# Logarithms first in the common ScalarE stretch: reordering one round of a fused RWKV, Mish and routed-expert kernel

## The chip, the cores and the metric

The kernel runs on one core of a Trainium2 chip. Its time is the device time of one execution in microseconds (us). A kernel's figure is the median of its timed runs. One further execution was recorded by the hardware profiler, and every row below comes from that one.

The engines in the rows are PE (TensorE, matmul), PEld (its weight loads), DVE (VectorE), ACT (ScalarE), POOL (GpSimd) and SP (SyncE, which issues most DMAs). Each works through its own instructions strictly in the order in which they stand in the program, and they meet only at semaphores.

## The reference

Three layers follow each other. The sizes are batch 4, 8 heads, sequence 768, head size 48, so 3072 tokens of 384 numbers.

```python
# 1. attention with a decaying state
for t in range(S):
    cur = np.einsum('bhd,bhe->bhde', u[None] * kt, vt)
    y[:, :, t] = np.einsum('bhd,bhde->bhe', rt, state + cur)
    state = wt[:, :, :, None] * state + np.einsum('bhd,bhe->bhde', kt, vt)
# 2. a dense layer of 2048 with h * tanh(softplus(h)) between
h = x @ w_in
sp = np.where(h > 20.0, h, np.log1p(np.exp(np.minimum(h, 20.0))))
x = (h * np.tanh(sp)) @ w_out
# 3. 8 experts, each token to one, at most 384 per expert, greedy by logit
logits = x @ w_gate
out[mask] = np.maximum(x[mask] @ w1[e], 0.0) @ w2[e]
```

## The kernel before

**Tiling.** The attention works on 24 units of 128 columns (two chunks of 64 tokens). The dense layer works on 12 groups g of 256 tokens, two units each. A group's first matmul (`mm1`) has 8 slots of 18 matmuls; each slot fills one PSUM tile `Hp`, and there are two of these. ScalarE takes a slot out of PSUM twice: as a sigmoid into `es` and scaled into `hs`. A few of the `hs` copies are on VectorE. The second matmul (`mm2`, into `X`) is cut into parts of three matmuls, and the number of parts that go into a slot stands in a list (`beat`).

**The activation.** tanh(softplus(h)) is made from the sigmoid by an arctangent over half a group (`act_ln`, 128x2048) and a sine over each quarter (`act_tanh`, 128x1024). VectorE multiplies the sine into `hs` (L594, the sine product). Then `act_g` splits the product into two halves of 16 bits, `ghi` (copy) and `glo` (rest, L607), which `mm2` reads.

**The attention unit.** Steps of unit n, each a function: `att0` multiplies up the decay along the tokens (a scan into `E`) and makes `rk`; `att_inv` forms 1/E on ScalarE as Ln and Exp; `att1` scales r; `att1b` improves the inverse by one Newton step and scales k by it (L410, L411 and L414, the result is `k1` and lies in the tile `T`); `att_K` transposes k1 on PE (L447) and copies it to `kn`; `att_A` multiplies k1 by r1 and the state by r1 (L430, L436) and a predicated copy puts the first into `Dt`; `att_S` makes the new state from `kn` (L465, L472, L474); `att4` closes the output (L487) and writes it split into `xg` (hi on ScalarE, lo on VectorE, L494), which `mm1` of a later group reads. `bon1` and `bon2` make the diagonal term with small matmuls.

**The order.** No scheduler decides it. Every step gets a number from `CFG`, the steps are sorted by it, and each engine's instructions stand in that order. Slot t has its `mm1` at t + 0.7 and its `mm2` parts at t + 1.275. In the middle of the kernel one group is one round of 8 slots; T stands for the number of a round's first slot. At T both halves of the group just finished have their sines in one place, which is called the common stretch here, and the Ln and Exp of two units stand there too. ScalarE evaluates functions from a table, and an ACT_TABLE_LOAD changes the table. The sigmoid and the arctangent share one table in this order, the sine takes another, and Ln and Exp a third. `att_inv` asks for its table for each unit. Nine of the ten common stretches (groups 1 to 9) hold Ln and Exp of two units, the tenth (group 10) none.

The buffers that matter: `hs` and `es` are two half-group tiles each, `E` two tiles (one per unit in turn), `Hp` two PSUM banks, `Y` (transposes, states, diagonal terms) two, and `A` one.

Of the kernel before, what the change touches and what calls it, by code (L numbers as in the profile page):

```python
# [9 lines left out]
F32 = mybir.dt.float32  # L10
F16 = mybir.dt.float16
I32 = mybir.dt.int32
AF = mybir.ActivationFunctionType
ALU = mybir.AluOpType
# [4 lines left out]
P = 128  # L19
# [4 lines left out]
CFG = {'conv': [-27.9, -26.2, -0.2, 0.8, 1.8, 2.8, 3.7, 5.3, 5.9, 6.6, 7.3, 8.0, 8.7, 10.4, 10.6, 11.3],  # L24
 'split': [-27.3, -25.6, 0.9, 1.9, 2.9, 3.8, 4.7, 5.6, 6.7, 7.4, 8.1, 8.8, 9.0, 11.2, 11.4, 12.1],
 'ogT': [7.4, 8.45, 9.9, 10.25, 10.95, 11.85, 12.55, 12.75],
 'ogM': [8.15, 9.35, 10.2, 10.9, 11.35, 11.95, 12.75, 13.95],
 'u': ({'att0': -3.6, 'bon1': -2.6, 'bon2': -1.6, 'inv': 0.22, 'r1': 0.23, 'k1': 0.24, 'K': 2.6, 'A1': 2.8,
        'S': 3.99, 'y': 4.0},
       {'att0': -1.5, 'bon1': -0.6, 'bon2': 1.6, 'inv': 0.25, 'r1': 0.26, 'k1': 3.1, 'K': 4.4, 'A1': 4.6,  # L30
        'S': 5.79, 'y': 5.8}),
 'un': {0: {'att0': -17.25,
            'inv': -16.75,
            'r1': -16.55,
# [53 lines left out]
            'k1': 4.3,  # L88
            'K': 5.9,
            'A1': 6.2,  # L90
            'S': 7.45}},
 'rate': [(9, 0), (16, 19), (80, 195), (82, 200), (85, 216), (89, 218), (93, 234), (99, 258)],
 'beat': (16, 80, (5, 4, 2, 2, 2, 1, 1, 5)),
 'close_cv': 15.0,
 'close_att': 86.65,
 'mm1': 0.7,
# [1 line left out]
 'aln': -0.1,  # L98
 'tanh': (1.475, 1.66),
 'g': (3.0, 3.0725),  # L100
 'both': (((0.1, 0.11), (0.105, 0.115)), ((0.12, 0.13), (3.2, 3.6))),
 'begin': {('warm', 0): -32,
           ('wg',): 5.6,
           ('ld', 4): -23.99,
# [66 lines left out]
         'ghi': {2, 6} | {i for i in range(8, 46) if i % 4 != 3},  # L171
         'hs': {64, 17, 55, 60, 63},
         'rk': {0, 1, 2, 3, 5, 6, 7, 9, 10, 11, 12, 13, 14, 15, 16, 17, 18, 19, 20, 21, 22, 23},
         'x0': set(),
         'bT': {22},
         'wT': {4}},
 'nd0': 8,
 'lg2': 4.725,
 'alone': {9},
 'lg': 4.51,  # L180
 'hold': 30}


# [1 line left out]
def tile_rwkv_mish_greedy_moe(  # L185
# [12 lines left out]
    nc = tc.nc  # L198
    NU, C, H, D = v.shape
    L = C // 2  # L200
# [4 lines left out]
    NP = H // 2  # L205
    F2 = w1.shape[2] * P // DM
    KD = DM // P
    NF = FF // P
    NS = NF // 2
    NF2 = F2 // P  # L210
    G = 256
    NG = NT // G
# [5 lines left out]
    SX, SWI, SG, SWO = 2.0**14, 2.0**10, 2.0**13, 2.0**11  # L218
# [16 lines left out]
    pm = p_moe.__enter__()  # L235
    pa = p_att.__enter__()
    pc = p_cv.__enter__()
# [68 lines left out]
    right = const.tile([P, 1], F32, name="right")  # L306
# [4 lines left out]
    first = pa.tile([P, 2 * NP, L + 1], F32, name="first", bufs=1)  # L311
    nc.gpsimd.memset(first, 0.0)
    nc.gpsimd.memset(first[:, :, 0:1], 1.0)
    full = pa.tile([P, P], I32, name="full", bufs=1)
    nc.gpsimd.memset(full, 1)
    nc.gpsimd.affine_select(out=full, in_=full, pattern=[[1, P]], compare_op=ALU.is_gt, fill=0,
                            base=0, channel_multiplier=-1)
# [16 lines left out]
    made = set()  # L334

    def need(*keys):
        assert made.issuperset(keys), keys

    def on_v(what, i):
        return i in CFG["dve"].get(what, ())  # L340

    def move(what, i, dst, src, scale=1.0):
        if on_v(what, i):
            nc.vector.tensor_scalar(dst, src, scale, None, op0=ALU.mult)
        else:
            nc.scalar.activation(dst, src, AF.Copy, scale=scale)  # L346

    def E_of(n):
        return E_buf[n % 2]
# [19 lines left out]
    def att_inv(n):  # L369
        need(("att0", n))  # L370
        inv = pa.tile([P, 2 * NP, L], F32, name="inv", bufs=2)
        if n > 1:
            nc.scalar.preload_act_table_set("natural_log_exp_and_others")
        nc.scalar.activation(inv, E_of(n)[:, :, 1:], AF.Ln)
        nc.scalar.activation(inv, inv, AF.Exp, scale=-1.0)
        st[n] = inv
# [29 lines left out]
    def att1b(n):  # L406
        E = E_of(n)
        inv, r1 = st[n]
        nt = pa.tile([P, 2 * NP, L], F32, name="nt", bufs=1)
        (nc.vector if on_v("nt", n) else nc.gpsimd).tensor_tensor(nt, inv, E_of(n)[:, :, 1:], op=ALU.mult)  # L410
        nc.vector.scalar_tensor_tensor(inv, nt, 2.0, inv, op0=ALU.subtract, op1=ALU.mult)  # L411
        k1 = Tps["k", n]
        kk = k1.rearrange("q p (h t) -> q (p h) t", h=2)
        nc.vector.scalar_tensor_tensor(kk, inv, -1.0, kk, op0=ALU.mult, op1=ALU.mult)  # L414
        st[n] = (k1, r1, None)
        made.add(("k1", n))
# [140 lines left out]
    hs, es, gs = {}, {}, {}  # L557
    HALF = NF // 4

    def mm1(g, j):  # L560
        need(("w", j), ("y", MG * g), ("y", MG * g + MG - 1))
        hf, q = divmod(j, HALF)
        if q == 0:
            hs[g, hf] = pm.tile([P, NF // 2, G], F32, name="hs", bufs=2)
            es[g, hf] = pm.tile([P, NF // 2, G], F32, name="es", bufs=2)
        made.add(("mm1", g, hf, q))
        h = pp.tile([P, 2, G], F32, name="Hp", bufs=2)
        for fi in range(2):
            f = 2 * j + fi
            n = 0  # L570
            for kk in range(KD):
                for a, b in ((0, 0), (0, 1), (1, 0)):
                    nc.tensor.matmul(h[:, fi, :], wi[:, a, kk, f * P:(f + 1) * P], xg[g][:, b, kk, :],  # L573
                                     start=(n == 0), stop=(n == 3 * KD - 1))
                    n += 1
        nc.scalar.activation(es[g, hf][:, 2 * q:2 * q + 2, :], h, AF.Sigmoid, scale=-1.0 / (SX * SWI))  # L576
        move("hs", g * NS + j, hs[g, hf][:, 2 * q:2 * q + 2, :], h, SG / (SX * SWI))

    def act_ln(H_):
        e = es[divmod(H_, 2)]  # L580
        need(("mm1", *divmod(H_, 2), HALF - 1))
        made.add(("at", H_))
        nc.scalar.activation(e, e, AF.Arctan)  # L583

    def act_tanh(H_, q):
        key = divmod(H_, 2)
        sl = slice(q * NF // 4, (q + 1) * NF // 4)
        h, e = hs[key][:, sl], es[key][:, sl]
        need(("at", H_))
        made.add(("sin", H_, q))  # L590
        if q == 0 and not (H_ % 2 and 0 < H_ // 2 < NG - 1):
            nc.scalar.preload_act_table_set("trig_and_small")
        nc.scalar.activation(e, e, AF.Sin, scale=-2.0, bias=right)  # L593
        nc.vector.tensor_tensor(h, h, e, op=ALU.mult)  # L594

    def act_g(H_, q):
        key = divmod(H_, 2)
        if q == 0:
            pool = pg3[0] if key[0] >= NG - 2 else (p_g, pg2[0])[key[0] // 2 % 2]
            gs[key] = pool.tile([P, 2, NF // 2, G], F16, name="g")  # L600
        gt = gs[key]
        made.add(("g", *key, q))
        need(("sin", H_, q))
        sl = slice(q * NF // 4, (q + 1) * NF // 4)
        h = hs[key][:, sl]
        move("ghi", 2 * H_ + q, gt[:, 0, sl], h)
        (nc.vector if on_v("glo", 2 * H_ + q) else nc.gpsimd).tensor_tensor(gt[:, 1, sl], h, gt[:, 0, sl], op=ALU.subtract)  # L607

# [78 lines left out]
    def at(key, f, *args):  # L687
        events.append((key, len(events), f, args))
# [4 lines left out]
    for f in range(NF):  # L693
        at(CFG["ogT"][f // 2], og_T, f)
        if f % 2 == 0:
            at(CFG["ogM"][f // 2], og_M, f)
    steps = {"att0": att0, "bon1": bon1, "bon2": bon2, "inv": att_inv, "r1": att1, "k1": att1b, "A1": att_A, "K": att_K, "S": att_S, "y": att4}
    for n in range(NU):
        own = CFG["un"].get(n)
        t0 = 8 * (n // 2) - 8 if own is None else 4 * n - 13  # L700
        for nm, o in (CFG["u"][n % 2] if own is None else own).items():
            at(t0 + o, steps[nm], n)
    nc.sync.dma_start(wg.rearrange("p k e -> p (k e)"), w_gate)
    warm_rhs = first.rearrange("p a c -> p (a c)").bitcast(F16)[:, 0:512]
# [50 lines left out]
    for t in range(NSLOT + 3):  # L755
        if t < NSLOT:
            at(t + CFG["mm1"], mm1, t // NS, t % NS)
        at(t + CFG["mm2"], mm2, t)
    for h in range(NSLOT // 4):
        t = 4 * h + 4  # L760
        at(t + CFG["aln"], act_ln, h)
        tanh, g = CFG["tanh"], CFG["g"]
        if 0 < h // 2 < NG - 1:
            t = 8 * (h // 2) + 8
            tanh, g = CFG["both"][h % 2]
        for q in range(2):
            at(t + tanh[q], act_tanh, h, q)
            at(t + g[q], act_g, h, q)
        if h % 2 and ND0 <= h // 2 < NG - 1:
            at(t + CFG["lg"], logits, h // 2)  # L770
            at(t + CFG["lg2"], logits_sum, h // 2)
# [16 lines left out]
    for i, o in enumerate(OFF + [1.0]):  # L788
        t = pgt.tile([P, J], F32, name=f"jk{i}")
# [32 lines left out]
    y = pgt.tile([P, NTT], F32, name="y")  # L822
# [215 lines left out]
    sl = pgt.tile([P, NTT], I32, name="sl")  # L1038
# [269 lines left out]
```

## Time and profile before

| what | us |
|---|---|
| median of 3 runs | 928.54 (926.84 to 928.73) |
| profiled execution, whole | 925.72 |
| its span (the rows' time axis) | 924.0 |
| PE busy | 777.9 (84%) |
| VectorE busy | 541.5 (59%) |
| ScalarE busy | 473.8 (51%) |
| GpSimd busy | 64.2 (7%) |

The span is what all rows count from. The busy shares are means over stages with different limits: loading and the first groups (0 to 149 us), nine rounds with a common stretch that holds Ln and Exp (149 to 560), the last groups and the routing (to about 710), the experts (the rest). The granted clock of PE is given in shares of 2.4 GHz: 1.00 is full, 0.50 is 1.2 GHz.

### The profile page before, as it was taken

The page shows a single profiled execution, that of the slowest core. Times are in us where ns is not written, and L with a number is a line of the kernel's source. Part 1 is how long each engine was busy: PE and PEld are TensorE (multiplying, and loading weights), DVE is VectorE, ACT ScalarE, POOL GpSimd, SP SyncE. Part 2 cuts the span into 40 slices and gives each one's busy share as a digit, 9 for nine tenths or more (in the row PEclk, how much of TensorE's full clock was granted, in tenths as well). Part 3 has the DMA queues.
Part 4 walks back from the last instruction along what each step waited for, and adds up shares of the span by engine and source line. Part 5 has one row for each costly group of instructions (what it writes and reads, how often), then busy time and mean ns, then how long its engine had stood idle before and what let it go on. Part 6 is the DMA issues. An engine that isn't in the chain of part 4 may idle for free. (4 is left out here: it accounts for less than half of the span.)

```text
span 924.0 us, 20138 instructions
## 1 busy us (share of the span) xinstructions
PE 777.9 (84%) x8819; PEld 531.1 (57%) x8819; DVE 541.5 (59%) x946; ACT 473.8 (51%) x694; POOL 64.2 (7%) x102
## 2 busy tenths in 40 slices
PE   6873887787878888797979697999995999999997
PEld 3553665565656656565657475755554555555564
DVE  7799855556565655666656535267775455554430
ACT  3357966574747474847384836721101454554421
POOL 1000000000000000000000000100002022233311
PEclk8797999798979898989989899999997999999999
DMA  7840511303030303031302000040042455544300
GB/s 287 261 133 5 172 27 23 70 14 70 14 70 23 70 14 70 14 67 26 79 14 46 13 11 13 10 155 19 18 152 65 154 180 188 174 146 161 127 27 26
DMA packets 22220, 74.12 MB, mean 80 GB/s; under 512 B 4496, under 2 KB 13072, under 8 KB 20080
## 3 DMA queue, kind: packets, MB, share of 16 engines
q1 hardware_dynamic: 19056, 63.35, 23.3%
q0 software_dynamic: 3072, 9.44, 3.2%
q8 instruction: 71, 1.16, 0.5%
q14 instruction: 21, 0.17, 0.1%
HBM read 62.15 MB, written 9.44 MB: 77 GB/s over the span
## 5 line engine op out<-in xcount | busy, mean ns | idle before, releaser
L573 PE MATMUL Hp<-xg,wi 128*128 128x256 f16 x1728 | 229.2, 292 | 9.1 <-ACT hs L346 5.7
L621 PE MATMUL X<-wo,g 128*128 128x392 f16 (+1 forms) x1152 | 214.2, 330 | 0.6 <-ACT wT L346 0.6
L573 PEld LDWEIGHTS <-wi 128*128 128x128 f16 x1728 | 177.8, 105 | 47.4 <-issue 7.6
L576 ACT ACTIVATE es<-Hp 128x512 f32<-128x512 f32 x96 | 57.5, 599 | 168.5 <-PE Hp L573 168.4
L621 PEld LDWEIGHTS <-g 128*128 128x128 f16 x1152 | 106.4, 98 | 64.2 <-issue 1.4
L594 DVE TENSOR_TENSOR hs<-hs,es 128x1024 f32<-128x1024 f32 x48 | 57.5, 1221 | 83.4 <-ACT es L593 83.4
L1153 PE MATMUL Hp<-xe,a 128*128 128x384 f16 (+1 forms) x612 | 100.9, 316 | 6.4 <-DVE hT L1158 5.2
L1170 PE MATMUL X<-a,hT 128*128 128x384 f16 x576 | 97.2, 326 | 0.0
L1153 PEld LDWEIGHTS <-a 128*128 128x128 f16 x612 | 57.6, 97 | 48.2 <-issue 14.2
L1170 PEld LDWEIGHTS <-hT 128*128 128x128 f16 x576 | 56.4, 98 | 34.8
L447 PE MATMUL Y<-ident,T 128*128 128x128 f32 x88 | 19.0, 353 | 62.3 <-DVE T L414 54.9
L1158 DVE SCALAR_TENSOR_TENSOR hT<-Hp,hT 128x384 f16<-128x384 f32 x64 | 35.3, 552 | 46.6 <-ACT hT L1157 46.6
L1099 DVE SCALAR_TENSOR_TENSOR a<-stg,a 128x1024 f16<-128x1024 f32 (+4 forms) x56 | 59.6, 1065 | 3.3 <-ACT a L1096 2.7
L607 DVE TENSOR_TENSOR g<-hs,g 128x1024 f16<-128x1024 f32 x48 | 57.9, 1224 | 5.1 <-ACT g L346 4.0
L1096 ACT ACTIVATE a<-stg 128x1024 f16<-128x1024 f32 (+4 forms) x56 | 51.1, 926 | 6.6 <-DMA stg<-in_w_dram 6.6
L346 ACT ACTIVATE hs<-Hp 128x512 f32<-128x512 f32 x91 | 54.2, 596 | 0.1
L1173 ACT ACTIVATE or<-X 128x384 f32<-128x384 f32 x24 | 11.8, 491 | 81.3 <-issue 61.0
L447 PEld LDWEIGHTS Y<-ident,T 128*128 128x128 f32 x88 | 12.6, 178 | 69.5 <-DVE T L414 58.4
L593 ACT ACTIVATE es<-es,right 128x1024 f32<-128x1024 f32 x48 | 51.7, 1138 | 0.2
L1135 DVE SCALAR_TENSOR_TENSOR xe<-cn,xe 128x384 f16<-128x384 f32 x24 | 13.3, 555 | 60.8 <-ACT xe L1134 60.8
L1157 ACT ACTIVATE hT<-Hp 128x384 f16<-128x384 f32 x64 | 31.4, 491 | 32.6 <-PE Hp L1153 31.5
L583 ACT ACTIVATE es<-es 128x2048 f32<-128x2048 f32 x24 | 45.9, 1912 | 0.1
(194 smaller groups left out, 922.4 us busy)
## 6 DMA issues: line engine op xcount, KB each, us to landing
stg<-in_w_dram SPq DMA_DIRECT2D x16, 1536.0 KB, 7.3
T<-in_rkw_dram SPq DMA_DIRECT2D x42, 289.5 KB, 5.0
v<-in_v_dram SPq DMA_DIRECT2D x24, 192.0 KB, 2.9
raw<-in_w_out_dram SPq DMA_DIRECT2D x6, 768.0 KB, 4.6
x_dram<-x1o SPq DMA_DIRECT2D x48, 96.0 KB, 2.2
wo<-in_w_in_dram SPq DMA_DIRECT2D x4, 768.0 KB, 8.2
raw<-in_w_in_dram SPq DMA_DIRECT2D x2, 768.0 KB, 7.7
g<-in_w_in_dram SPq DMA_DIRECT2D x2, 768.0 KB, 10.5
```

The lines of the kernel that those rows point to most:

```text
L346: nc.scalar.activation(dst, src, AF.Copy, scale=scale)
L573: nc.tensor.matmul(h[:, fi, :], wi[:, a, kk, f * P:(f + 1) * P], xg[g][:, b, kk, :], start=(n == 0), stop=(n == 3 * KD - 1))
L576: nc.scalar.activation(es[g, hf][:, 2 * q:2 * q + 2, :], h, AF.Sigmoid, scale=-1.0 / (SX * SWI))
L583: nc.scalar.activation(e, e, AF.Arctan)
L593: nc.scalar.activation(e, e, AF.Sin, scale=-2.0, bias=right)
L594: nc.vector.tensor_tensor(h, h, e, op=ALU.mult)
L607: (nc.vector if on_v("glo", 2 * H_ + q) else nc.gpsimd).tensor_tensor(gt[:, 1, sl], h, gt[:, 0, sl], op=ALU.subtract)
L621: nc.tensor.matmul(x, gt[:, a, ff, m * P:(m + 1) * P], wo[:, b, f, 0:n], start=(f == 0 and i == 0), stop=(f == NF - 1 and i == 2))
L1096: nc.scalar.activation(dst[:, 0], src, AF.Copy, scale=sc_)
L1099: nc.vector.scalar_tensor_tensor(dst[:, 1], src, sc_, dst[:, 0], op0=ALU.mult, op1=ALU.subtract)
L1153: nc.tensor.matmul(ps[:, cs], a1[:, a, kk, f * P:(f + 1) * P], x[:, b, kk, cs], start=(n == 0), stop=(n == 3 * KD - 1))
L1170: nc.tensor.matmul(ps, h[:, a, f, ms], a2[:, b, f, :], start=(n == 0), stop=(n == 3 * NF2 - 1))
```

## The change

- In the common stretch the Ln and Exp of both units come first, on one table load; then one load of the sine's table, under which the arctangent of the second half now runs as well; then the four sines.
- On VectorE, `att1` and `att1b` of both units stand ahead of the four sine products. The products of the first half come next, those of the second half at T + 2.45 and T + 2.5, and the splits (`g`) are spread from T + 1.33 to T + 4.7.
- `att_K` and `att_A` of the first unit move from T + 2.6 and 2.8 (behind the second slot) to T + 1.28 and 1.3 (behind the first), its `att_S` and `att4` from about 4 to 2.4, and the second unit's steps from 4.4 to 5.8 to 3.3 to 4.6. `att0`, `bon1` and `bon2` of the next round's units move with them.
- `hs` becomes five tiles of a quarter group. To make room, the Newton product `nt` is written over the first 64 columns of `E`, and `full` goes to another pool.
- Five `hs` copies go from VectorE to ScalarE, most `kn` copies of even units from ScalarE to VectorE, and `beat` moves one `mm2` part from the second slot of a round to the sixth.

```diff
- 'u': ({'att0': -3.6, 'bon1': -2.6, 'bon2': -1.6, 'inv': 0.22, 'r1': 0.23, 'k1': 0.24, 'K': 2.6, 'A1': 2.8,
-        'S': 3.99, 'y': 4.0},
-       {'att0': -1.5, 'bon1': -0.6, 'bon2': 1.6, 'inv': 0.25, 'r1': 0.26, 'k1': 3.1, 'K': 4.4, 'A1': 4.6,
-        'S': 5.79, 'y': 5.8}),
+ 'u': ({'att0': -5.0, 'bon1': -3.1, 'bon2': -2.1, 'inv': 0.1, 'r1': 0.101, 'k1': 0.102, 'K': 1.28, 'A1': 1.3,
+        'S': 2.39, 'y': 2.4},
+       {'att0': -2.8, 'bon1': -1.9, 'bon2': -0.8, 'inv': 0.11, 'r1': 0.111, 'k1': 0.112, 'K': 3.3, 'A1': 3.4,
+        'S': 4.59, 'y': 4.6}),
...
- 'beat': (16, 80, (5, 4, 2, 2, 2, 1, 1, 5)),
+ 'beat': (16, 80, (5, 3, 2, 2, 2, 2, 1, 5)),
...
- 'both': (((0.1, 0.11), (0.105, 0.115)), ((0.12, 0.13), (3.2, 3.6))),
+ 'both': ((0.12, (0.14, 0.15), (1.33, 2.75)), (0.13, (2.45, 2.5), (3.6, 4.7))),
...
-        if n > 1:
+        if n > 1 and (n < 6 or n % 2 == 0):
             nc.scalar.preload_act_table_set("natural_log_exp_and_others")
...
-        nt = pa.tile([P, 2 * NP, L], F32, name="nt", bufs=1)
+        nt = E[:, :, 0:L]
...
         if q == 0:
-            hs[g, hf] = pm.tile([P, NF // 2, G], F32, name="hs", bufs=2)
             es[g, hf] = pm.tile([P, NF // 2, G], F32, name="es", bufs=2)
+        if q % 2 == 0:
+            hs[g, hf, q // 2] = pm.tile([P, NF // 4, G], F32, name="hs", bufs=5)
...
     def act_ln(H_):
         e = es[divmod(H_, 2)]
         need(("mm1", *divmod(H_, 2), HALF - 1))
         made.add(("at", H_))
+        if H_ % 2 and 0 < H_ // 2 < NG - 1:
+            nc.scalar.preload_act_table_set("trig_and_small")
         nc.scalar.activation(e, e, AF.Arctan)
...
+            at(t0 + sin, act_sin, h, 0, 1)
+            for q in range(2):
+                at(t0 + he[q], act_he, h, q)
+                at(t0 + g[q], act_g, h, q)
```

The next three places show what stands in a row on one engine, all of the round of group 6, which in the trace of before begins at 376.7 us. In the changed program the line numbers are a few higher (L594 becomes L605, L447 becomes L449).

ScalarE before, from the sigmoid of the group's last slot to the load that gives the sigmoid its table back:

```order
L576 ACTIVATE es<-Hp 128x512
L583 ACTIVATE es<-es 128x2048
L592 ACT_TABLE_LOAD
L593 ACTIVATE es<-es,right 128x1024 x4
L373 ACT_TABLE_LOAD
L374 ACTIVATE inv<-E_134 128x512
L375 ACTIVATE inv<-inv 128x512
L373 ACT_TABLE_LOAD
L374 ACTIVATE inv<-E_137 128x512
L375 ACTIVATE inv<-inv 128x512
L576 ACT_TABLE_LOAD
```

ScalarE of the changed program, the same place (`hs` is the copy that was on VectorE):

```order
L579 ACTIVATE es<-Hp 128x512
L348 ACTIVATE hs<-Hp 128x512
L375 ACT_TABLE_LOAD
L376 ACTIVATE inv<-E_134 128x512
L377 ACTIVATE inv<-inv 128x512
L376 ACTIVATE inv<-E_137 128x512
L377 ACTIVATE inv<-inv 128x512
L587 ACT_TABLE_LOAD
L588 ACTIVATE es<-es 128x2048
L597 ACTIVATE es<-es,right 128x1024 x4
L579 ACT_TABLE_LOAD
```

Four table loads become three, and both units' Ln and Exp stand ahead of the arctangent and the sines instead of behind them.

VectorE before, from the first sine product to the second unit's scaled r (T_89 and T_90 are the tiles of the two units):

```order
L594 TENSOR_TENSOR hs<-hs,es 128x1024
L344 TENSOR_SCALAR g<-hs 128x1024
L607 TENSOR_TENSOR g<-hs,g 128x1024
L594 TENSOR_TENSOR hs<-hs,es 128x1024
L344 TENSOR_SCALAR g<-hs 128x1024
L607 TENSOR_TENSOR g<-hs,g 128x1024
L594 TENSOR_TENSOR hs<-hs,es 128x1024 x2
L382 TENSOR_TENSOR T_89<-T_89,E_134 128x512
L410 TENSOR_TENSOR nt<-inv,E_134 128x512
L411 SCALAR_TENSOR_TENSOR inv<-nt,inv 128x512
L414 SCALAR_TENSOR_TENSOR T_89<-inv,T_89 128x512
L382 TENSOR_TENSOR T_90<-T_90,E_137 128x512
```

VectorE of the changed program, from the first unit's scaled r to the copy of its transposed k1:

```order
L384 TENSOR_TENSOR T_89<-T_89,E_134 128x512
L412 TENSOR_TENSOR E_134<-inv,E_134 128x8x64
L413 SCALAR_TENSOR_TENSOR inv<-E_134,inv 128x512
L416 SCALAR_TENSOR_TENSOR T_89<-inv,T_89 128x512
L384 TENSOR_TENSOR T_90<-T_90,E_137 128x512
L412 TENSOR_TENSOR E_137<-inv,E_137 128x8x64
L413 SCALAR_TENSOR_TENSOR inv<-E_137,inv 128x512
L416 SCALAR_TENSOR_TENSOR T_90<-inv,T_90 128x512
L605 TENSOR_TENSOR hs<-hs,es 128x1024 x2
L346 TENSOR_SCALAR x1o<-X 128x384
L640 TENSOR_SCALAR V<-X 128x8
L346 TENSOR_SCALAR kn<-Y 128x512
```

The three instructions of each unit's k1 stand ahead of all sine products, and `kn` stands behind two of them.

PE before, at the transposes of the first unit's k1 (12 `mm2` matmuls stand ahead of them, 18 `mm1` matmuls behind):

```order
L621 LDWEIGHTS g
L621 MATMUL X<-wo,g 128x392
L447 MATMUL Y<-ident,T_89 128x128 x4
L573 LDWEIGHTS wi
L573 MATMUL Hp<-xg,wi 128x256
```

PE of the changed program, at the same transposes, which stand one slot earlier:

```order
L449 MATMUL Y<-ident,T_89 128x128 x4
L432 MATMUL A<-T_89 64x64 x16
L438 MATMUL A<-T_89,S_135 64x64 x16
L576 LDWEIGHTS wi
L576 MATMUL Hp<-xg,wi 128x256
```

The products `A` now follow the transposes directly, and the next `mm1` is that of the round's second slot instead of its third.

## Rows read from the trace of the kernel before

**Rows 1.** Waits of PE, 148 to 560 us: total us, times, longest

```profile
PE Y L447 <- DVE T L414: 54.9, 9, 7.8
```

**Rows 2.** Round of group 6 and all nine: length, engines' busy us, clock, DMA

```profile
379.28:423.80 44.52, 36.44 (x510) 27.14 (x509) 29.52 (x43) 26.66 (x37) 1.33 (x1) 0.92 0.23 48
...
sum 411.03, PE 331.24 PEld 246.12 DVE 238.47 ACT 250.66 POOL 1.33; mean PE 36.80 PEld 27.35 DVE 26.50 ACT 27.85 POOL 0.15
```

**Rows 3.** Timeline of ScalarE, round of group 6: start, us, instruction, idle before

```profile
377.35 1.91 ACT L583 ACTIVATE es<-es 128x2048 f32<-128x2048 f32 x1
...
380.57 4.27 ACT L593 ACTIVATE es<-es,right 128x1024 f32<-128x1024 f32 x4
384.86 1.28 ACT L373 ACT_TABLE_LOAD   x1
386.15 0.63 ACT L374 ACTIVATE inv<-E 128x512 f32<-128x512 f32 x1
...
387.46 1.28 ACT L373 ACT_TABLE_LOAD   x1
...
391.36 0.60 ACT L576 ACTIVATE es<-Hp 128x512 f32<-128x512 f32 x1
391.86 0.59 ACT L346 ACTIVATE hs<-Hp 128x512 f32<-128x512 f32 x1
```

**Rows 4.** Timeline of PE, same round

```profile
376.52 2.65 PE L621 MATMUL X<-wo,g 128*128 128x392 f16 x15
379.01 2.13 PE L573 MATMUL Hp<-xg,wi 128*128 128x256 f16 x18
380.97 2.65 PE L621 MATMUL X<-wo,g 128*128 128x392 f16 x15
...
393.07 1.12 PE L447 MATMUL Y<-ident,T 128*128 128x128 f32 x4 [5.39 <-DVE T L414]
393.98 4.05 PE L573 MATMUL Hp<-xg,wi 128*128 128x256 f16 x18
397.96 0.80 PE L430 MATMUL A<-T 48*64 48x64 f32 x32
...
399.16 1.17 PE L621 MATMUL X<-wo,g 128*128 128x392 f16 x6
...
402.22 0.68 PE L465 MATMUL Y<-v,kn 64*64 64x48 f32 x32
402.73 0.63 PE L487 MATMUL A<-Dt,v 64*48 64x64 f32 x32
...
418.70 0.43 PE L392 MATMUL Y<-rk,u_T 128*32 128x64 f32 x16 [0.78 <-DVE rk L366]
```

**Rows 5.** Timeline of VectorE, same round

```profile
381.75 1.23 DVE L594 TENSOR_TENSOR hs<-hs,es 128x1024 f32<-128x1024 f32 x1 [3.71 <-ACT es L593]
...
383.74 1.23 DVE L607 TENSOR_TENSOR g<-hs,g 128x1024 f16<-128x1024 f32 x1
...
390.88 0.69 DVE L410 TENSOR_TENSOR nt<-inv,E 128x512 f32<-128x512 f32 x1
...
405.01 0.61 DVE L472 TENSOR_TENSOR S<-S,Y 128x192 f32<-128x192 f32 x2
...
406.13 0.75 DVE L494 SCALAR_TENSOR_TENSOR xg<-A,xg 128x256 f16<-128x256 f32 x2
406.79 0.68 DVE L344 TENSOR_SCALAR kn<-Y 128x512 f32<-128x512 f32 x1
407.39 1.23 DVE L363 TENSOR_TENSOR_SCAN E<-T,first 128x520 f32<-128x520 f32 x1
...
409.12 0.72 DVE L438 COPY_PREDICATED Dt<-mask,A 128x512 f32<-128x512 int32 x1
```

**Rows 6.** PE in single microseconds: length, busy (instructions), clock, DMA share, GB/s

```profile
180.00:181.00 1.00, 1.00 (x26) 0.50 0.47 107
...
391.00:392.00 1.00, 0.00 (x0) 0.71 0.00 0
...
404.00:405.00 1.00, 0.46 (x3) 1.00 0.51 123
```

More of the change, by code (lines that the diff above doesn't have):

```diff
@@ L90 @@
             'A1': 6.2,
-            'S': 7.45}},
+            'S': 7.45},
+        6: {'att0': -3.6, 'bon1': -2.7, 'bon2': -0.9},
+        7: {'att0': -1.4, 'bon1': -0.6, 'bon2': -0.4}},
  'rate': [(9, 0), (16, 19), (80, 195), (82, 200), (85, 216), (89, 218), (93, 234), (99, 258)],
- 'beat': (16, 80, (5, 4, 2, 2, 2, 1, 1, 5)),
+ 'beat': (16, 80, (5, 3, 2, 2, 2, 2, 1, 5)),
  'close_cv': 15.0,
@@ L168 @@
          'Dt': {0, 1, 2, 3, 4, 5, 6, 7, 8, 9, 10, 11, 12, 13, 14, 15, 16, 18, 19, 20, 21, 22, 23},
[1 row of a table removed]
[1 row of a table added]
          'x1': {2, 3, 5, 7, 8},
-         'ghi': {2, 6} | {i for i in range(8, 46) if i % 4 != 3},
-         'hs': {64, 17, 55, 60, 63},
+         'ghi': {2} | {i for i in range(4, 46) if i % 4 != 3},
+         'hs': set(),
          'rk': {0, 1, 2, 3, 5, 6, 7, 9, 10, 11, 12, 13, 14, 15, 16, 17, 18, 19, 20, 21, 22, 23},
@@ L177 @@
  'nd0': 8,
- 'lg2': 4.725,
+ 'lg2': 5.2,
  'alone': {9},
- 'lg': 4.51,
+ 'lg': 4.9,
  'hold': 30}
@@ L313, in tile_rwkv_mish_greedy_moe @@
     nc.gpsimd.memset(first[:, :, 0:1], 1.0)
-    full = pa.tile([P, P], I32, name="full", bufs=1)
+    full = pc.tile([P, P], I32, name="full", bufs=1)
     nc.gpsimd.memset(full, 1)
@@ L576, in mm1 @@
         nc.scalar.activation(es[g, hf][:, 2 * q:2 * q + 2, :], h, AF.Sigmoid, scale=-1.0 / (SX * SWI))
-        move("hs", g * NS + j, hs[g, hf][:, 2 * q:2 * q + 2, :], h, SG / (SX * SWI))
+        move("hs", g * NS + j, hs[g, hf, q // 2][:, 2 * (q % 2):2 * (q % 2) + 2, :], h, SG / (SX * SWI))
     def act_ln(H_):
@@ L582, in act_ln, with act_sin, act_he @@
         made.add(("at", H_))
+        if H_ % 2 and 0 < H_ // 2 < NG - 1:
+            nc.scalar.preload_act_table_set("trig_and_small")
         nc.scalar.activation(e, e, AF.Arctan)
-    def act_tanh(H_, q):
[L586 to L594, printed above, removed]
+    def act_sin(H_, *qs):
+        need(("at", H_))
+        both = 0 < H_ // 2 < NG - 1
+        for q in qs:
+            e = es[divmod(H_, 2)][:, q * NF // 4:(q + 1) * NF // 4]
+            if q == 0 and not both:
+                nc.scalar.preload_act_table_set("trig_and_small")
+            nc.scalar.activation(e, e, AF.Sin, scale=-2.0, bias=right)
+            made.add(("sin", H_, q))
+    def act_he(H_, q):
+        need(("sin", H_, q))
+        made.add(("he", H_, q))
+        sl = slice(q * NF // 4, (q + 1) * NF // 4)
+        h, e = hs[(*divmod(H_, 2), q)], es[divmod(H_, 2)][:, sl]
+        nc.vector.tensor_tensor(h, h, e, op=ALU.mult)
+    def act_tanh(H_, q):
+        act_sin(H_, q)
+        act_he(H_, q)
     def act_g(H_, q):
@@ L602, in act_g @@
         made.add(("g", *key, q))
-        need(("sin", H_, q))
+        need(("he", H_, q))
         sl = slice(q * NF // 4, (q + 1) * NF // 4)
-        h = hs[key][:, sl]
+        h = hs[(*key, q)]
         move("ghi", 2 * H_ + q, gt[:, 0, sl], h)
@@ L698, in tile_rwkv_mish_greedy_moe @@
     for n in range(NU):
-        own = CFG["un"].get(n)
-        t0 = 8 * (n // 2) - 8 if own is None else 4 * n - 13
-        for nm, o in (CFG["u"][n % 2] if own is None else own).items():
+        t0 = 8 * (n // 2) - 8 if n >= 6 else 4 * n - 13
+        for nm, o in {**(CFG["u"][n % 2] if n >= 6 else {}), **CFG["un"].get(n, {})}.items():
             at(t0 + o, steps[nm], n)
@@ L760, in tile_rwkv_mish_greedy_moe @@
         t = 4 * h + 4
[L761 to L768, printed above, removed]
+        both = 0 < h // 2 < NG - 1
+        at(t + (0.115 if both and h % 2 else CFG["aln"]), act_ln, h)
+        if both:
+            t0 = 8 * (h // 2) + 8
+            sin, he, g = CFG["both"][h % 2]
+            at(t0 + sin, act_sin, h, 0, 1)
+            for q in range(2):
+                at(t0 + he[q], act_he, h, q)
+                at(t0 + g[q], act_g, h, q)
+        else:
+            for q in range(2):
+                at(t + CFG["tanh"][q], act_tanh, h, q)
+                at(t + CFG["g"][q], act_g, h, q)
         if h % 2 and ND0 <= h // 2 < NG - 1:
```

2 rows, old and new, of the table CFG are left out of this document.

## The prediction

> **What bounds the kernel now.** I read four views: the table of rounds, PE's waits, then one round on ScalarE, PE and VectorE in order of time, and PE's clock in single microseconds.
>
> The nine rounds whose common stretch holds Ln and Exp take 411.0 us together, and the one of group 6 takes 44.5 [rows 2]. PE is busy for 331 of the 411 and is nearest to full, so the question is what it waits for. One wait dominates: the transposes of k1 wait for the Newton step on VectorE, 54.9 us in nine waits, one per round [rows 1].
>
> The round of group 6 shows how it arises. ScalarE starts the arctangent at 377.35, the sines at 380.57, a load at 384.86, the first unit's Ln at 386.15, a second load at 387.46, and takes the next `Hp` at 391.36 [rows 3]. VectorE can start the Newton step only at 390.88 [rows 5]. PE runs out of work at 387.7 and starts the transposes at 393.07, after 5.39 us of idling [rows 4]. The clock falls between 391 and 392 us, when PE has issued nothing for over three microseconds [rows 6]. So the first `mm1` after the wait takes 4.05 us where others take 2.13 [rows 4]. The wait and the clock cost some 7.8 us a round (5.4, 1.9 on `mm1`, 0.5 on the transposes).
>
> But k1 is not the only gate. `mm1` behind the transposes needs an `Hp` tile that ScalarE frees only after the stretch, at about 392.4 (391.86 plus 0.59) [rows 3]. With k1 there long before, that `mm1` could start at 392.4 instead of 393.98, no sooner. What the change can win depends on the length of the stretch and on how much work PE finds inside it.
>
> **The change part by part.** I walk group 6's round with the durations of its rows. Zero is the end of `mm1` of the last slot before the stretch (376.67; its sigmoid starts at once).
>
> ScalarE: sigmoid and copy take 1.1 (391.36 to 391.86 plus 0.59) [rows 3]. A load is 1.28 plus a gap of 0.01, Ln and Exp of a unit 1.31 (386.15 to 387.46), the arctangent 1.91, four sines 4.27 [rows 3]. In the new order: load to 2.4, first unit's Exp done at 3.75, second's at 5.1, load to 6.35, arctangent to 8.3, sines to 12.55, load to 13.8, first slot out of PSUM at 14.9. One load of 1.29 is saved per round, 11.6 us over nine; the stretch sets the end of a round only in part, so I do not add this separately.
>
> On what a load costs: the first load for Ln starts at 384.86 as the sines end at 384.84, and Ln follows 1.29 later [rows 3]. The Trainium skill, "ScalarE: Activation LUTs", section "What ACT_TABLE_LOAD costs", gives 1283 ns for the load and another 1380 ns of drain for every switch. The trace agrees on the load and shows no drain. With the page's drain nine loads fewer would be worth 12 us more; I use the row.
>
> VectorE: the Newton step starts at 3.8, and k1 stands 2.2 later (390.88 to 393.07) [rows 4, 5], at 6.0; the second unit's k1 at 8.7. The first sine product can start 1.18 after the first sine (380.57 to 381.75) [rows 3, 5], at 9.45, so both k1 fit in ahead of it at no cost: VectorE only waited there (3.71 before the product) [rows 5]. Then in its new order: two products of 1.23 to 11.9, x1o and V (taken like one copy, 0.65) to 12.5, `kn` 0.68 to 13.2, the predicated copy 0.7 to 13.9, the first split 2.0 (copy and rest; product to rest 1.99, rest 1.23) to 15.9, the state 1.1 (405.01 to 406.13) to 17.0, `xg` 0.7 to 17.7, two products to 20.1, a split to 22.1, scan and `rk` 1.7 (407.39 to 409.12) to 23.8, `kn` to 24.5, predicated copy to 25.2, split to 27.2, state to 28.3, `xg` to 29.0, rest to 30.2, scan and `rk` to 31.9 [rows 5].
>
> PE: 15 matmuls of `mm2` cost 2.49 (376.52 to 379.01), one `mm1` 1.96 (379.01 to 380.97), the transposes 0.55 at full clock (0.91 at half), the products A 1.2 (397.96 to 399.16), the state 0.5, y 0.6 [rows 4].
> - `mm2` to 2.3, `mm1` of slot T to 4.3, `mm2` to 6.8. k1 is there since 6.0, so the transposes go at once, to 7.35; A to 8.55; `mm1` T+1 to 10.5; nine `mm2` matmuls to 12.0.
> - State waits for `kn` (13.2), to 13.8; y for the predicated copy, to 14.5; `mm1` T+2 for `Hp` (14.95), to 16.9.
> - Six `mm2` matmuls to 17.9, second transposes 18.5, A 19.7, `mm1` T+3 21.7, `mm2` 22.7. The second state waits for `kn` (24.5), to 25.1; y to 25.8.
> - `mm1` T+4 to 27.8, `bon1` 0.4 [rows 4], `mm2` 29.2, `mm1` T+5 31.1. The second `bon1` waits for `rk` (31.9), as it waits 0.78 now [rows 4]; to 32.4. `mm2`, `mm1` T+6, `mm2`, `mm1` T+7 end at 38.0.
>
> So the round becomes 38.0 against 44.5. PE still idles 4.3 of it, the longest wait being 1.8 for the second `kn`.
>
> Bounds for what the trace does not show. Nothing here runs `nt` over `E`; as one pass over 128x512 it is taken at its present 0.69, and one microsecond each way would not reach the product at 9.45. The quarter tiles of `hs`: the copy of slot T+2 at 16.9 plus 0.5 needs the first split's end at 15.9, which hides it by 1.5; with that cover gone ScalarE stands and PE behind it (rival 4). The five `hs` copies on ScalarE cost 0.5 each ahead of a stretch, counted in the 1.1. SP's loads for later units move with y: the new y stands earlier in its round, so they can only be earlier.
>
> The clock: gaps shorter than today's do not all spare it. Between 404 and 405 PE is busy for 0.46 and keeps 1.00, but at 180 to 181 it runs at 0.50 after two waits of under 1 us [rows 6]. A fall costs at most the 1.9 of one `mm1` at half clock. Below nothing it cannot go; above, two falls a round make 3.8. I take half a fall, 1.0, nearer to the row that kept its clock. That is 39.0 a round.
>
> Sum: 411.0 - 9 x 39.0 = 60.0 saved. The mean round before is 45.7, longer than group 6's, because the first rounds have more waits of the same kind. The profiled execution (924.0 of span and 1.7 around it) becomes 865.7. The median of the runs lies 2.8 higher, at 928.5, so the forecast is 868. Outside the nine rounds I count nothing: the tenth stretch keeps its two loads and has no unit.
>
> **The rivals.**
> 1. The clock falls every round. The gaps at 12 to 15 and 22.7 to 25.8 lie among small matmuls. For it: 180 to 181; against it: 404 to 405 [rows 6]. One fall a round is 0.9 x 9 = 8 us more than I took, two are 2.8 x 9 = 25; I price it between them, at 17: 885. The Trainium skill, "TensorE: Matmul & The Clock Gate", section "A second HAM failure mode: psum-queue depth-cycling", says that frequent short idles between groups of matmuls are enough to make the clock swing. By that rule this rival is the likelier; the trace bears it out in some rounds only.
> 2. VectorE becomes the bound. Its queue from 9.45 to 31.9 has no gap in the walk, and it is busy 29.5 of the round now [rows 2]. If each of PE's three waits for it (1.2, 1.8, 0.7) grows by 1 us, a round takes 42: 895. Against it: before and behind that queue it has some 6 us of slack.
> 3. The stretch alone counts. If the attention's steps are still late (A waits for the state or the `A` bank of the round before), only the earlier `Hp` is left: 14.95 against 17.3 (393.98 less 376.67), 2.4 a round: 907.
> 4. Slower: the five `hs` tiles turn into a lock. Slot T+2's copy waits for the first split, which stands behind `kn` and the predicated copy, which wait for PE's transposes and A. It costs from a split that ends after 17.4 and decides once it ends after 25 (the 7.7 a round between 38.0 and the mean round of 45.7); ending at 25.8 it costs 0.7 x 9 more than before: 935. Against it: A is done at 8.55.
> 5. The gain is larger: without any fall and with the waits a third shorter (1.5 of 4.3) a round takes 36.5: 846.
>
> **How the numbers follow.** Forecast 0.60 (38 to 40 a round, 858 to 878), rival 1 0.15, rival 2 0.10, rival 3 0.07, rival 4 0.03, rival 5 0.05. The range for 8 in 10 runs from 848 to 892 and leaves out rivals 3 and 4 and parts of 2 and 5. A measurement tells some 0.2% (1.9 us) from no change. Only rival 4 lies above: slower 0.03; same 0.02, taken from rival 3's tail; faster 0.95.
>
> **What would show it.** The waits of the first transposes for k1 are gone in all nine rounds. ScalarE's stretch, from its first load to its last one's end, is 12.7. The clock holds 1.00 through it. PE's remaining waits are for `kn`, for `Hp` and for `rk`, together 4 to 5 us a round. Rounds are 38 to 40 long. The forecast is wrong if transposes still wait over 2 us, if `mm1` of 4 us remain in most rounds, or if ScalarE waits for a split before an `hs` copy.

## The result

The changed kernel takes 870.25 us (median of four runs, 869.81 to 871.51) against 928.09 for the kernel before, a ratio of 0.9381 with a 95% interval from 0.9364 to 0.9397. The forecast was 868. The profiled execution took 869.97, its span is 868.3 against 924.0.

**Waits of PE.** The one large wait of [rows 1] is gone. This is PE's list over the whole span (total us, times, longest):

```profile
PE Y L467 <- DVE kn L346: 15.1, 11, 3.9
PE Y L394 <- DVE rk L368: 11.0, 7, 1.6
PE Hp L576 <- ACT hs L348: 10.7, 7, 4.5
...
PE Y L449 <- DVE T L416: 0.5, 1, 0.5
```

The transposes (L449 now) wait for k1 once, for 0.5 us, where they waited 54.9. In its place stand three smaller waits, for `kn`, `rk` and `Hp` (the longest of these, 4.5 for `Hp`, lies behind the nine rounds).

**Rounds.** These are the rounds of groups 1, 5, 6, 8 and 9, each from the first table load of its stretch (columns as in [rows 2]; the clock is the third number from the end):

```profile
147.88:184.70 36.82, 33.05 (x504) 25.43 (x502) 26.36 (x38) 26.20 (x38) 0.00 (x0) 1.00 0.23 53
...
297.00:337.85 40.85, 35.40 (x510) 26.81 (x508) 26.26 (x38) 26.30 (x38) 1.04 (x1) 0.96 0.24 47
337.85:375.91 38.06, 34.05 (x510) 26.12 (x508) 28.56 (x43) 25.33 (x37) 0.00 (x0) 1.00 0.25 57
...
414.01:457.39 43.38, 37.69 (x563) 28.52 (x561) 27.48 (x42) 26.35 (x37) 0.00 (x0) 0.96 0.15 31
457.39:500.76 43.37, 38.44 (x512) 28.70 (x510) 21.02 (x31) 25.76 (x35) 0.00 (x0) 0.96 0.06 13
```

The nine take 352.9 us (147.88 to 500.76) where they took 411.0, which is 58.1 less. Six of them are short (36.8 to 38.1) and hold the clock at 1.00; three are long (40.9, 43.4, 43.4) and lose the clock in part. Group 6 is 38.06 against 44.52.

**ScalarE.** The x1o of group 5's round (x1o is the copy of a finished `mm2` tile `X` out of PSUM), then the stretch of group 6, answering to [rows 3]:

```profile
310.42 0.50 ACT L348 ACTIVATE x1o<-X 128x384 f32<-128x384 f32 x1
...
337.85 1.28 ACT L375 ACT_TABLE_LOAD   x1
...
340.34 0.62 ACT L376 ACTIVATE inv<-E 128x512 f32<-128x512 f32 x1
...
341.64 1.28 ACT L587 ACT_TABLE_LOAD   x1
342.93 1.92 ACT L588 ACTIVATE es<-es 128x2048 f32<-128x2048 f32 x1
344.75 4.25 ACT L597 ACTIVATE es<-es,right 128x1024 f32<-128x1024 f32 x4
349.01 1.28 ACT L579 ACT_TABLE_LOAD   x1
```

From the first load to the last one's end the stretch lasts 12.44 us.

**PE.** First the state of group 5's round with the `mm1` behind it, then group 6 (answers to [rows 4]):

```profile
311.77 0.68 PE L467 MATMUL Y<-v,kn 64*64 64x48 f32 x32 [3.88 <-DVE kn L346]
...
313.00 3.80 PE L576 MATMUL Hp<-xg,wi 128*128 128x256 f16 x18
...
343.49 0.60 PE L449 MATMUL Y<-ident,T 128*128 128x128 f32 x4
...
349.47 0.68 PE L467 MATMUL Y<-v,kn 64*64 64x48 f32 x32 [0.73 <-DVE kn L346]
...
351.44 2.12 PE L576 MATMUL Hp<-xg,wi 128*128 128x256 f16 x18 [0.66 <-ACT hs L348]
...
360.19 0.68 PE L467 MATMUL Y<-v,kn 64*64 64x48 f32 x32 [1.04 <-DVE kn L346]
...
366.85 0.27 PE L400 MATMUL Y<-ident,bT 128*128 128x128 f32 x1
368.70 0.43 PE L394 MATMUL Y<-rk,u_T 128*32 128x64 f32 x16 [1.58 <-DVE rk L368]
```

**VectorE.** The same two rounds (answers to [rows 5]):

```profile
310.95 0.17 DVE L640 TENSOR_SCALAR V<-X 128x8 f32<-128x8 f32 x1 [3.52 <-ACT x1o L348]
311.03 0.68 DVE L346 TENSOR_SCALAR kn<-Y 128x512 f32<-128x512 f32 x1
...
340.47 0.69 DVE L412 TENSOR_TENSOR E<-inv,E 128x512 f32<-128x512 f32 x1 [8.68 <-ACT inv L377]
...
363.66 0.75 DVE L496 SCALAR_TENSOR_TENSOR xg<-A,xg 128x256 f16<-128x256 f32 x2
365.68 1.23 DVE L622 TENSOR_TENSOR g<-hs,g 128x1024 f16<-128x1024 f32 x1 [1.27 <-ACT g L348]
```

The new thing is the first row. V, a copy of the eight gate logits that stand beside x1o in the same tile, starts only when ScalarE has done x1o, though both only read that tile; why it has to, the rows do not show. In this round x1o is on ScalarE, behind the stretch, so VectorE stands for 3.52 us with `kn` queued behind V; PE's state waits 3.88, the clock falls, and the next `mm1` takes 3.80. Group 8's round shows the same 3.88, group 9's 2.24.

### The profile page after: what moved, and what is told of

The parts are those of the page before. It is cut to its first block, busy times and chain, and to the rows that moved or that the text cites. A ratio compares the mean times of both kernels' runs of the same rounds, so it can differ in the third digit from the quotient of the medians.

```text
span 868.3 us, 20153 instructions
## 1 busy us (share of the span) xinstructions
PE 757.0 (87%) x8819; PEld 521.7 (60%) x8819; DVE 542.5 (62%) x949; ACT 456.4 (53%) x682; POOL 63.8 (7%) x102
## 5 line engine op out<-in xcount | busy, mean ns | idle before, releaser
L576 PE MATMUL Hp<-xg,wi 128*128 128x256 f16 x1728 | 211.3, 278 | 12.4 <-ACT hs L348 10.7
L576 PEld LDWEIGHTS <-wi 128*128 128x128 f16 x1728 | 169.1, 100 | 42.9 <-issue 11.1
L605 DVE TENSOR_TENSOR hs<-hs,es 128x1024 f32<-128x1024 f32 x48 | 56.7, 1220 | 29.8 <-ACT es L597 29.8
L622 DVE TENSOR_TENSOR g<-hs,g 128x1024 f16<-128x1024 f32 x48 | 58.6, 1225 | 22.4 <-ACT g L348 21.3
L348 ACT ACTIVATE hs<-Hp 128x512 f32<-128x512 f32 x96 | 57.1, 595 | 0.0
L348 ACT ACTIVATE x1o<-X 128x384 f32<-128x384 f32 x19 | 9.3, 491 | 71.3 <-issue 60.1
L412 DVE TENSOR_TENSOR E<-inv,E 128x512 f32<-128x512 f32 x23 | 15.9, 692 | 40.5 <-ACT inv L377 39.2
```

## The experiments

Each kernel is the changed one with the edit shown, unless said otherwise. A ratio is to the kernel before.

**k1 behind sine products again.** It undoes one part, VectorE's order: k1 of both units stands behind the first two of the four sine products.

```diff
-'inv': 0.1, 'r1': 0.101, 'k1': 0.102,
+'inv': 0.1, 'r1': 0.151, 'k1': 0.152,
-'inv': 0.11, 'r1': 0.111, 'k1': 0.112,
+'inv': 0.11, 'r1': 0.153, 'k1': 0.154,
```

> The changed kernel with one part undone: VectorE's steps r1 and k1 of both units stand behind the first two sine products again; ScalarE's order, the places of PE's steps and the buffers stay. Theory (the early k1 on VectorE fills PE's time inside the stretch): the transposes wait for k1 until two products and the Newton step are done, some 14.7 us behind the zero of the walk instead of 6.8; a round grows by 6 to 8 us and PE's clock falls again, so 925 to 945, the whole gain gone. Rival (the shorter stretch on ScalarE carries the gain): at most 2 us a round, 870 to 890.

Measured: 932.27, ratio 1.0056 (1.0042 to 1.0071). PE in the round of group 5 (columns as in [rows 4]):

```profile
341.28 1.11 PE L449 MATMUL Y<-ident,T 128*128 128x128 f32 x4 [7.44 <-DVE T L416]
```

The wait for k1 is back, at 7.44, and the transposes take 1.11 where they took 0.60, with a granted clock of 0.50 (341 to 344 us). The whole gain is gone and 5 us with it, although ScalarE keeps its shorter stretch. The theory holds.

**The attention's steps at their old places.** k1 stays early; only the places of att0, bon1, bon2, K, A1, S and y go back (the second unit's bon2 to -0.5, not to its old 1.6).

```diff
-'K': 1.28, 'A1': 1.3, 'S': 2.39, 'y': 2.4
+'K': 2.6, 'A1': 2.8, 'S': 3.99, 'y': 4.0
-'K': 3.3, 'A1': 3.4, 'S': 4.59, 'y': 4.6
+'K': 4.4, 'A1': 4.6, 'S': 5.79, 'y': 5.8
...
```

> The changed kernel with another part undone: the attention's steps (att0, bon, K, A1, S, y) of both units stand at their old places again, behind the second and third slot, while k1 stays early on VectorE and the Ln and Exp first on ScalarE. Theory (what fills PE inside the stretch is the moved work, k1 is only what allows it): PE has no work from about 10.3 us behind the walk's zero until Hp comes free at 14.9, so a wait of 4 to 5 us for Hp in each round and often a fall of the clock; 3 to 6 us a round, 895 to 920. Rival (k1's readiness is all that matters, PE catches up later in the round): 870 to 880.

Measured: 914.33, ratio 0.9864 (0.9848 to 0.9880). PE in the round of group 4:

```profile
285.49 0.60 PE L449 MATMUL Y<-ident,T 128*128 128x128 f32 x4
289.99 3.79 PE L576 MATMUL Hp<-xg,wi 128*128 128x256 f16 x18 [3.91 <-ACT hs L348]
```

k1 is in time and the transposes run, but then PE has nothing until `Hp` comes free, and the clock falls. Over the rounds PE waits 38.0 us for `Hp` in nine waits. So an early k1 without the moved steps keeps 13 of the 57 us (0.0136 of 927); 45 (0.0483) hang on the places of the steps. Not all of that is the stretch: the products `A` now wait 14.1 us for `xg` in eight waits, which the changed kernel does not have in these rounds.

**The second table load back.**

```diff
-        if n > 1 and (n < 6 or n % 2 == 0):
+        if n > 1:
```

> The changed kernel with the second unit's table load put back between the two units' Ln and Exp: nine loads more, everything else as it is. Theory (the stretch's end decides, since sine products, kn and the first Hp all come from it): each load costs 0.9 to 1.3 us, 8 to 12 us in all, so 878 to 882. Rival 1 (PE's work covers the load): 0 to 3 us, 870 to 873. Rival 2 (a load also drains the engine for 1.4 us, as the Trainium skill, ScalarE: Activation LUTs, section What ACT_TABLE_LOAD costs, has it for a switch): 2.7 us a round, 894.

Measured: 887.95, ratio 0.9592 (0.9569 to 0.9614), some 18 us more for nine loads, above the theory's 8 to 12 and below the 24 of rival 2. ScalarE at one such load, and the rounds of groups 1, 2 and 4:

```profile
268.41 0.63 ACT L377 ACTIVATE inv<-inv 128x512 f32<-128x512 f32 x1
269.06 1.28 ACT L375 ACT_TABLE_LOAD   x1
270.35 0.63 ACT L376 ACTIVATE inv<-E 128x512 f32<-128x512 f32 x1
```

```profile
148.81:188.65 39.84, 34.65 (x504) 26.18 (x502) 26.52 (x38) 27.58 (x39) 0.00 (x0) 0.96 0.22 49
188.65:227.51 38.86, 34.00 (x510) 26.11 (x508) 27.32 (x40) 27.20 (x38) 0.00 (x0) 1.00 0.26 50
...
266.45:305.28 38.83, 34.01 (x510) 26.09 (x508) 26.86 (x39) 27.20 (x38) 0.00 (x0) 1.00 0.25 51
```

The load starts as Exp ends and Ln follows 1.29 later; no idle time of 1.4 us shows on either side. Groups 2 and 4 grow by 1.4 us (from 37.44 and 37.42), which is the load plus the 0.12 by which the second Ln otherwise overlaps the first Exp. So does group 7 (38.10 to 39.52). In these rounds, which keep their clock, the stretch passes on in full what it grows by; nine times 1.4 is 12.7 of the 16.9 us that the nine rounds grow. Group 1 grows by 3.0, with its clock at 0.96 instead of 1.00: its `mm1` behind the stretch takes 3.69. Group 3 has as slow an `mm1` (3.79) and grows by only 1.5, so a fall of the clock does not always cost the round its whole size.

**One load less in the kernel before.** The same line the other way, in the kernel before, nothing moved.

> The kernel before with one thing changed: the second unit's table load is left out where the table is already there, nine loads less, nothing moved. Theory (there the transposes wait for k1 behind four sine products on VectorE, not for ScalarE, so a shorter stretch is worth nothing until k1 is moved): within 2 us of the kernel before. Rival (a load is worth what it costs in e3_load_back, 1.4 us and more each): 12 to 17 us less, 910 to 915.

Measured: 926.55, ratio 1.0002 (0.9991 to 1.0013). PE in one round:

```profile
391.51 1.11 PE L447 MATMUL Y<-ident,T 128*128 128x128 f32 x4 [6.11 <-DVE T L414]
```

The wait is still for VectorE. The same nine loads are worth nothing there and 18 us in the new order.

**x1o of three tiles on VectorE.**

```diff
-         'x1': {2, 3, 5, 7, 8},
+         'x1': {2, 3, 5, 6, 7, 8, 10, 11},
```

> The changed kernel, with the x1o evictions of three tiles (6, 10 and 11) on VectorE instead of ScalarE. In the trace of the changed kernel VectorE waits 3.52 us (groups 5 and 8) and 1.13 us (group 9) in front of the small copy V until ScalarE has done x1o, which stands behind the stretch; kn and with it PE's state stand behind that (3.88, 3.88 and 2.24 us of waiting, then mm1 at half clock). Theory (the wait for x1o makes these three rounds long): the waits for kn shrink to below 1 us, mm1 behind them takes 2.1 us, the round of group 5 comes down from 40.85 to 37 to 38 us, and the time falls by 6 to 10 us, to 860 to 864. Rival (these rounds are long because of Hp or of more mm2 work in them): within 2 us of 870.

Measured: 868.51, ratio 0.9362 (0.9347 to 0.9377), not told apart from the changed kernel, so the time is the rival's. The rounds of groups 5 and 8, then PE in the latter, then its clock:

```profile
298.78:336.22 37.44, 34.00 (x510) 26.11 (x508) 26.63 (x39) 25.82 (x38) 1.04 (x1) 1.00 0.25 52
412.38:455.77 43.39, 39.72 (x563) 29.49 (x561) 27.90 (x43) 25.85 (x37) 0.00 (x0) 0.92 0.15 31
```

```profile
424.00 0.68 PE L467 MATMUL Y<-v,kn 64*64 64x48 f32 x32 [0.73 <-DVE kn L346]
...
439.62 1.05 PE L663 MATMUL Hp<-g,wo 128*8 128x256 f16 x32 [1.11 <-ACT g L348]
440.88 0.28 PE L663 MATMUL Hp<-g,wo 128*8 128x256 f16 x4 [0.21 <-DVE g L622]
441.65 1.02 PE L675 MATMUL Hp<-pick,lgt 128*128 128x8 f32 x4 [0.49 <-ACT lgt L348]
...
444.44 4.05 PE L576 MATMUL Hp<-xg,wi 128*128 128x256 f16 x18
```

```profile
441.00:442.00 1.00, 0.51 (x6) 0.80 0.15 31
442.00:443.00 1.00, 1.00 (x6) 0.50 0.02 2
```

In group 5 the theory holds: the wait for `kn` is now 0.72, and the round falls from 40.85 to 37.44. Group 8 wins nothing. Its wait for `kn` is 0.73 and the middle of the round is 4.0 us shorter, but 0.7 of that goes around a new wait of 0.47 for the predicated copy and 3.3 to the clock, which now falls later, after three short waits among the logits (1.3 ahead of `mm1`, and `mm1` takes 4.05). In the changed kernel the same three waits (1.11, 0.21 and 0.48) had left the clock at 1.00:

```profile
446.00:447.00 1.00, 0.52 (x8) 1.00 0.10 18
```

Group 9 gives the theory no support: its wait for `kn` is still 1.49, the `mm1` behind it is slow as before, and the round takes 43.24 against 43.37. In part the rival is right for groups 8 and 9. In the next run, where these two and group 6 all hold 1.00, PE is busy for 36.4 and 37.0 us in them and for 34.0 in group 6. Both hold 53 matmuls of the separate logits, whose places the change also moved (`lg` from 4.51 to 4.9, `lg2` from 4.725 to 5.2).

**Four `hs` tiles instead of five**, with the x1o edit as well, to be compared with the run above.

```diff
-            hs[g, hf, q // 2] = pm.tile([P, NF // 4, G], F32, name="hs", bufs=5)
+            hs[g, hf, q // 2] = pm.tile([P, NF // 4, G], F32, name="hs", bufs=4)
```

> As e1_x1_vector, but with four quarter tiles of hs instead of five, to be compared with e1_x1_vector. Theory (the ring of five is what lets the splits be spread): the copies of the slots T and T+2 must wait for the splits of the quarters four before, which end about 1 us and 4 to 5 us after them; ScalarE stands and mm1 waits for Hp, 4 to 6 us a round and half a fall of the clock, so 40 to 60 us over e1_x1_vector. Rival (the splits are done in time anyway): within 3 us of e1_x1_vector.

Measured: 869.93, ratio 0.9408 (0.9382 to 0.9433), 1.4 us more in the medians and 4 by the ratio, which one run of 875.96 draws up. The theory's 40 to 60 us fell. ScalarE and PE in the round of group 4, then the rounds of groups 5 and 8:

```profile
281.63 0.60 ACT L348 ACTIVATE hs<-Hp 128x512 f32<-128x512 f32 x1 [3.61 <-DVE g L622]
```

```profile
275.26 2.12 PE L576 MATMUL Hp<-xg,wi 128*128 128x256 f16 x18 [1.79 <-ACT hs L348]
...
284.62 2.14 PE L576 MATMUL Hp<-xg,wi 128*128 128x256 f16 x18
```

```profile
299.08:337.63 38.55, 34.01 (x510) 26.10 (x508) 26.72 (x39) 25.81 (x38) 1.04 (x1) 1.00 0.23 50
...
415.71:456.90 41.19, 36.42 (x563) 27.81 (x561) 27.94 (x43) 25.84 (x36) 0.00 (x0) 1.00 0.16 33
```

The copy of slot T+2 does wait, for 3.61 us (4 to 5 were worked out), but PE does not: its next `mm1` has the other `Hp` tile, and the one behind that starts at 284.62, after the copy is done. Only the 0.5 us at slot T's copy reaches PE (1.79 instead of the 1.2 in the same round of the run above). That is not nothing: each round of groups 1 to 7 is 0.6 to 1.2 us longer than in the run above, 6.0 together. The times still agree because group 8 holds its clock here (41.19 against 43.39) and the first round begins at 147.0 instead of 149.7, so the near-equal times are in part luck.

**The second bon1 later**, on top of the x1o edit.

```diff
-'bon1': -1.9, 'bon2': -0.8, 'inv': 0.11,
+'bon1': -1.25, 'bon2': -0.7, 'inv': 0.11,
```

> e1_x1_vector with the second unit's bon1 one step later in PE's order (behind the mm1 of the round's seventh slot, its bon2 behind the mm2 that follows). In the trace of the changed kernel this bon1 waits 1.58 us for rk in seven of the nine rounds. Theory (PE's order sets that wait, and PE bounds the end of a round): seven waits of 1.58 us go, 8 to 11 us less than e1_x1_vector, 858 to 861. Rival (the wait is taken up again by the next wait in the same round, for Hp or for kn): within 3 us of 868.

Measured: 857.68, ratio 0.9251 (0.9237 to 0.9265), 10.8 us less than without it. The round of group 5, then PE in the round of group 6:

```profile
294.54:330.93 36.39, 34.15 (x510) 26.02 (x508) 26.62 (x39) 25.81 (x37) 1.04 (x1) 1.00 0.27 53
```

```profile
364.50 0.33 PE L400 MATMUL Y<-ident,bT 128*128 128x128 f32 x1 [0.38 <-ACT bT L348]
```

The time is the theory's (seven waits of 1.58 are 11.1), but it is not made up as the theory has it. Each of the seven rounds falls by 1.05 us, as group 5 from 37.44 to 36.39, 7.4 together: two thirds of the wait were on PE's path, and a new wait of 0.38 for `bT` takes part of the rest. Another 2.4 come from groups 8 and 9, which had no such wait and whose clock is better here (0.96 for 0.92, 1.00 for 0.96).

**Two more on top**: `kn` and the predicated copy ahead of the first sine products, and the separate logits later.

```diff
-'both': ((0.12, (0.14, 0.15), (1.33, 2.75)),
+'both': ((0.12, (1.31, 1.32), (1.33, 2.75)),
-'lg2': 5.2, 'lg': 4.9,
+'lg2': 6.3, 'lg': 5.8,
```

> e6_bon_later, and two more: kn and the predicated copy ahead of the first two sine products on VectorE (they wait 0.2 to 1.5 us behind them now, and PE's state waits for kn), and the separate logits of groups 8 to 10 behind the mm1 of the round's sixth slot (they wait some 1.8 us inside for the last split). Theory (each of these waits is on PE's path and the clock holds 1.00 once they are short): 4 to 8 us less than e6_bon_later, 850 to 857. Rival (the stretch's end, which frees Hp, decides the middle of the round: a wait that goes from kn comes back in front of mm1 as a wait for Hp): no more than 3 us less than e6_bon_later.

Measured: 855.82, ratio 0.9239 (0.9227 to 0.9252). PE's waits from 146 to 515 us, first without the two edits, then with them:

```profile
PE Hp L576 <- ACT hs L348: 12.6, 10, 4.5
PE Y L467 <- DVE kn L346: 8.0, 11, 1.4
```

```profile
PE Hp L576 <- ACT hs L348: 23.5, 10, 4.5
...
PE Y L467 <- DVE kn L346: 2.1, 2, 1.1
```

The rival holds: the wait for `kn` shrinks by 5.9 and that for `Hp` grows by 10.9. The middle of the round is set by the end of the stretch. The 1.9 us by which the medians differ are not clear of the intervals. The later logits may still be worth something: group 8's is the only round that falls clearly (42.37 to 40.06), while those of groups 3, 5 and 6 grow by 0.5 to 0.6. This version is the fastest of all, 13 to 14 us below the changed kernel.

## Why the prediction was right

The forecast of 868 rested on a walk through one round, and that round came out at the length walked: 38.06 against 38.0. With zero at 336.7 (the end of the last slot's `mm1`), the transposes were to start at 6.8 and started at 6.8; `mm1` T+2 at 14.95 and at 14.7; the second `bon1` at 31.9 and at 32.0. The removed wait, the full clock through the stretch and the three new waits (4.0 us in this round, forecast 4 to 5) are all there. Both halves were needed: with k1 late nothing is left, with the steps late 13 us. The smaller parts (the moved `mm2` part, the copies that change engine, the places of the logits) were not undone one by one.

The sum met the result partly by luck, because errors cancelled.

- **The clock's allowance** (1.0 us in every round, 39.0 a round) has the right mean, 352.9 / 9 = 39.2, and the wrong shape. Six rounds hold 1.00 and average 37.5; three average 42.5; only two of the nine lie in the 38 to 40 that was to show it. Rival 1 (a fall every round) did not come, but its mechanism is real: three rounds lose the clock. The bound of 1.9 for a fall is too low, since matmuls beside the `mm1` slow down too: the run with x1o moved lost 3.3 us to one fall.
- **"x1o and V (taken like one copy, 0.65)"** is the step that failed in group 5, for 3.4 us. It held for group 6, where x1o is on VectorE. In groups 5, 8 and 9 x1o is on ScalarE, V waits for it, and `kn` stands behind V. I walked one round and counted it nine times; the place of x1o was in the list of what runs on VectorE. Groups 8 and 9 have more work for PE than the walked round as well, and they stayed at 43.4 and 43.2 when x1o was moved; how their 5.3 us over group 6 divide was not settled.
- **The wait for `rk`** was walked at 0.7 and is 1.58, though `rk` came when walked. VectorE was 1.3 us ahead of the walk at `xg` (its end at 27.7 instead of 29.0) and lost that again, because the last split's second half (L622) waits 1.27 for its first half on ScalarE, which I had counted as done. PE came 0.7 earlier than walked (the end of L400 at 30.4 instead of 31.1), and so waits longer. That the round ends at 38.06 is owed to this cancelling: with `bon1` later it takes 37.01.
- **Ln and Exp of the first unit** take 1.2, not 1.31, since the second Ln overlaps the first Exp, and the first sine starts 0.1 before the arctangent's end. The stretch is 12.44 against 12.7.
- **The profiled execution and the median.** The forecast had 865.7 for the profiled execution and 2.8 more for the median. The profiled execution took 869.97, 4.3 more (1.9 of it in the rounds, the rest outside them), and the median lies only 0.3 above it. So 2.5 of the 4.3 were hidden.
- **Outside the nine rounds** I counted nothing. The changed kernel begins its first round 1.0 us later and spends 1.4 more behind the last. The start of the first round lies between 147.9 and 149.7 in three kernels that are alike up to there (the changed one, the one with the load back and the one with x1o moved), so the first of these is within scatter; the second was not followed up.
- **Rival 4** (the `hs` ring as a lock) had the wait right and its reach wrong: two `Hp` tiles stand between ScalarE's wait and PE. Two half-group tiles with the new spread of the splits were not tried.

## What to carry to other kernels

When an engine waits at a stretch of another engine, ask both what releases it and what it could do meanwhile: here an early release without the moved work kept 13 of 57 us, and a shorter stretch alone nothing. What an operation is worth depends on the order around it, so the same nine table loads were 0 us in one order and 18 in another. In a strict queue look at the small instructions that stand ahead of an urgent one, in every round and not in one, since a copy of eight numbers per row held up `kn` by 3.5 us. And compare the rounds, not only the time: twice here a time met what was expected of it while the rounds showed another make-up.

## What the runs showed of the hardware

A table load costs its 1.28 us also when the table is already there (the load at 269.06 above), and ScalarE stands for only 0.02 us before it and 0.01 behind it. PE's clock fell after three waits of 1.11, 0.21 and 0.49 us within some three microseconds, and held 1.00 behind the same three waits in the changed kernel, and through waits of 0.73 and 0.66 in the stretch. In the kernel before it fell after two waits of 0.94 and 0.95 us (0.50 at 180 us [rows 6]). So the waits just before do not by themselves tell whether the clock falls; which of them costs it moves from round to round with edits elsewhere.
